# Mixture of experts between attention and a cosine MLP: second-layer product two blocks behind, PSUM split five and three, three float64 blocks in the last stage

## Chip, cores and metric

The kernel runs on one core of a Trainium2 chip. The metric is the device time of one execution in microseconds, the median over several runs. A separate profiled execution gives the trace.

## The reference, cut to what matters

Three layers one after the other: attention with a position bias, a mixture of eight experts of which every token uses two, and an MLP with a cosine gate. The last two are what the change touches.

```python
# x: 1152 tokens x 512, after attention
out = np.zeros((N, D), dtype=np.float32)
for e in range(E):                       # E = 8
    for k in range(2):
        mask = top2[:, k] == e
        h = np.maximum(x[mask] @ w1[e], 0.0)           # 512 -> 1024
        out[mask] += top2_w[mask, k, None] * (h @ w2[e])   # 1024 -> 512

def _moe2_ref(x, w_in, w_out):           # 512 -> 2048 -> 512, weights float64
    h = x @ w_in
    g = h * np.cos(h)
    return (g @ w_out).astype(np.float32)
```

## The kernel before, in words

**Stages.** Attention fills the first 240 us. Its tokens go to DRAM (`xg`) in eight slots of C = 320 rows, one slot for each expert. The function `experts` then does the experts' stage and the last stage. It exists in several copies for different numbers of tokens in the fullest expert; the one that ran uses W = 304 columns.

**Products.** Every matrix is split in two parts, a high part (hi) in the matmul's own 32-bit format (float32r) and a remainder (lo), and a product is three matmuls, hi x hi, hi x lo and lo x hi (`passes`, L990, matmul at L996). A split is a copy on ScalarE, which rounds, and a subtraction on VectorE or GpSimd. So each block of weights (128 x 1024) costs L1034 and L1036, each token tile L1100 and L1102, and the hidden layer L1125 and L1127 (`hhl`).

**Experts' stage.** A block is 128 of an expert's 1024 hidden units; 8 experts have 64 blocks. For block g, `ejobs` (L1111) makes l1, 12 matmuls into one PSUM bank H; relu and split into `hhl`; then l2, 12 matmuls that add into four banks Y, which hold the expert's 512 outputs for W tokens. l2 has priority g+1.5, one block behind l1. After the last block the four Y are transposed into the one tile `io` (L1147) and stored to DRAM (`yd`, L1151). The tokens of an expert come from `xg` into the same tile `io` (L1088), are transposed (L1097) and split into `xhl`, which has two buffers (`xjobs`, L1085). So `io` holds in turn the tokens of expert e+1, the result of e, the tokens of e+2.

**Weights.** `wjobs` (L1014) loads a block into one of three `raw` tiles and splits it into a `whl` tile, of which there are four: three that were split during attention (shown as `qt` in the rows) and one of its own.

**Last stage.** The tokens are three groups of three tiles of 128. For each group `mjobs` (L1196) goes over 16 blocks: m1 (12 matmuls of 384 columns into an H bank), the cosine on ScalarE and VectorE as a chain of seven instructions (L1236 to L1248), and m2 (three matmuls of 512 columns for each tile, into its Y bank), two blocks behind m1 (priority 2.5). Before a group, `cjobs` (L1156) gathers each token's two results with GpSimd, weighs and adds them, and transposes them through an H bank (L1185).

**The float64 blocks.** The weights of the last stage come as float64. `djobs` (L1040) loads a block of 1024 KB into the tile `r64`, of which there is one (L1045), and makes a float32 from the two words of each number, in two halves: a ScalarE copy (L1060), three VectorE instructions (L1062, L1064, L1066), then the split, L1068 on ScalarE and L1070 on VectorE or GpSimd. The first `NPRE` = 12 blocks are made during the experts' stage and kept in tiles `w64`; the other four are made in the last stage's first group, after the gathers of that group, into the `whl` tiles, and stay there for all three groups.

**Order.** Nothing is ordered by hand. `Plan` (L55) takes each operation with its engine or engines and a duration for each, a priority, and what it reads and writes, and places them as a list scheduler: of the operations that could start within 0.08 us of the earliest, the lowest priority number goes first, on the engine where it would end first. What has a limited number of buffers opens them in the order of priority (`turn`). The resulting order is the program's; on the chip each engine and each DMA queue runs its own list in that order and waits for semaphores. All loads and stores here are issued by the queue of SP but for GpSimd's gathers.

Of the kernel before, what the change touches and what calls it, by code (L numbers as in the profile page):

```python
# [8 lines left out]
F32 = mybir.dt.float32  # L9
# [10 lines left out]
DM = H * D  # L20
# [16 lines left out]
RAWS = 3  # L37
# [127 lines left out]
def attention_moe_cosine_mlp_kernel(  # L165
# [783 lines left out]
    def experts(bctx, W, ahead=True):  # L949

        pool = bctx.enter_context(tc.tile_pool(name="mlp", reuse_waits="tile", bufs=1))
        ps = bctx.enter_context(tc.tile_pool(name="ps", reuse_waits="tile", bufs=4, space=PSUM))
        bctx.enter_context(tc.manual_schedule())
        NPRE = 12
        FINE = {NFIRST: 1}
        DG, CF, CS = 2, 1, 3
        DP, FREE = 3, 0
        IDLE0, IDLE1 = 0, 0
# [6 lines left out]
        bufs = dict(Y=4, H=4, raw=RAWS, whl=4, xhl=2, hhl=3, io=1, r64=1, s=4, w=2, u=4)  # L965
# [3 lines left out]
        whls = wfirst + [pool.tile(sizes["whl"], F32R, name="whl")]  # L969
# [5 lines left out]
        def tl(tag, key):  # L975
            if (tag, key) not in live:
                if tag in "YH":
                    live[tag, key] = ps.tile([128, 512], F32, name=tag)
# [8 lines left out]
        def xhl(k, v):  # L987
            return xparts[k % 2][v]

# [24 lines left out]
        def wjobs(i, pr):  # L1014
# [6 lines left out]
            if i in FINE:  # L1021
                n = FINE[i]
                for a, c in [(0, c) for c in range(n)] + [(1, 0)]:
# [5 lines left out]
                    P.op({"DVE": 0.07 + 0.00104 * m, "POOL": 0.1 + 0.00225 * m}, (lambda a, sl: lambda e: (  # L1029
# [6 lines left out]
            P.op({"DVE": 1.135, "POOL": 2.0}, lambda e: (nc.gpsimd if e == "POOL" else nc.vector).tensor_tensor(  # L1036
# [3 lines left out]
        def djobs(f, pr, step, load_after=(), after=()):  # L1040
# [8 lines left out]
            for m in range(2):  # L1049
# [28 lines left out]
                P.op({"DVE": 0.602, "POOL": 1.25}, words(5), p + 0.05, r=[uk + (3,), wn + (0, m)], w=[wn + (1, m)])  # L1078
# [6 lines left out]
        def xjobs(e, pr):  # L1085
            ik = ("io", ("x", e))
            for i in range(4):
                xl.setdefault(e, []).append(P.op({"SP": 0.45}, (lambda i: lambda en: nc.sync.dma_start(  # L1088
                    tl(*ik)[32 * i:32 * i + 32].rearrange("p j c b -> p j (c b)"), blocked(xg, e, i)))(i),
                    pr - 2.5 - 2 + 0.01 * i, r=["xg"], w=[ik + (i,)], xfer=0.455))  # L1090
            for c in range(4):
# [3 lines left out]
                def part(u, c=c):  # L1095
# [3 lines left out]
                    pr - 2.5 + 0.4 * c, r=[ik + (i,) for i in range(4)], w=[sk])  # L1099
                P.op({"ACT": 0.093 + 0.00083 * W}, (lambda part, sk: lambda en: nc.scalar.activation(  # L1100
                    part(0), tl(*sk)[:, 0:W], AF.Copy))(part, sk), pr - 2.5 + 0.4 * c + 0.01, r=[sk], w=[xk + (0,)])
                P.op({"DVE": 0.402}, (lambda part, sk: lambda en: nc.vector.tensor_tensor(  # L1102
                    part(1), tl(*sk)[:, 0:W], part(0).bitcast(F32), op=OP.subtract))(part, sk),
                    pr - 2.5 + 0.4 * c + 0.02, r=[sk, xk + (0,)], w=[xk + (1,)])
# [6 lines left out]
        def ejobs(g):  # L1111
# [9 lines left out]
            for c0 in (0, 2):  # L1121
                ml1[-g] = P.op({"PE": 0.0025 * W}, l1(c0), g + 0.1 * c0, r=wuse(g, 0, (c0, c0 + 1))
                     + [("xhl", e, c, u) for c in (c0, c0 + 1) for u in range(2)], w=[pk + (c0,)], hold=[hk])
# [13 lines left out]
            for c in range(4):  # L1137
                P.op({"PE": 0.00125 * W}, l2(c), g + 1.5 + 0.01 * c, r=wuse(g, 1, (0,))
# [57 lines left out]
        def mjobs(g, f, pr):  # L1196
# [13 lines left out]
            for c0 in (0, 2):  # L1210
                ml1[g, f] = P.op({"PE": 0.0025 * N}, m1(c0), pr + 0.1 * c0 - (0 if (g, f) == (0, 0) else 0), r=[wn + (u, 0) for u in range(2)]
# [67 lines left out]
            for s in range(T):  # L1279
# [3 lines left out]
                for q in range(n):  # L1283
                    yk, c, d = ("Y", 4 * E + t + q), slice(DM // n * q, DM // n * (q + 1)), slice(0, DM // n)
                    P.op({"PE": 0.64 / n}, m2(s, yk, c, d), pr + 2.5 + 0.01 * s + 0.001 * q, r=[wn + (v, 1) for v in range(2)]
# [211 lines left out]
```

## Time and profile before

| what | value |
|---|---|
| median of 3 runs | 697.38 us (694.0 to 697.47) |
| profiled execution, its own time | 690.71 us |
| span of its trace | 688.9 us, 12810 instructions |
| TensorE busy | 634.7 us, 92% |
| VectorE busy | 505.3 us, 73% |
| ScalarE busy | 395.2 us, 57% |
| GpSimd busy | 137.0 us, 20% |
| mean granted TensorE clock | 0.981 of full speed |

The span runs from the first to the last instruction; 1.8 us lie around it. Busy shares are means over the stages. In the trace PE is TensorE's matmuls, PEld its weight loads, DVE VectorE, ACT ScalarE, POOL GpSimd, SP the queue that issues most DMAs. Ends of matmuls are modelled, so starts are the safer numbers.

### The profile page before, as it was taken

How to read it: one execution, taken by the hardware profiler on the slowest of the kernel's cores; microseconds unless marked ns; L12 is line 12 of the kernel's file. 1: busy time of each engine (PE TensorE's matmuls, PEld its weight loads, DVE VectorE, ACT ScalarE, POOL GpSimd, SP SyncE). 2: the span in 40 equal slices, each digit the busy share in tenths (PEclk: the TensorE clock that was granted, in tenths of full speed). 3: DMA queues.
4: the chain of work that ended last, by engine and by line, in shares of the span. 5: the costliest groups of instructions: out<-in, count | busy, mean ns of one | idle time of the engine just before them, and what ended most of it. 6: DMA issues, size and time to landing. Idle time of an engine off the chain costs nothing.

```text
span 688.9 us, 12810 instructions
## 1 busy us (share of the span) xinstructions
PE 634.7 (92%) x4678; PEld 552.6 (80%) x4678; DVE 505.3 (73%) x1256; ACT 395.2 (57%) x789; POOL 137.0 (20%) x196
## 2 busy tenths in 40 slices
PE   5778999999999859998999999999999999999996
PEld 1346676676688659998999998899999999999996
DVE  7796899999879529986888879556887545554543
ACT  5666688869668336664665656444664354334333
POOL 4140124332322202321122231022300040001000
PEclk9998999999999869999999999999999999999999
DMA  5858788776864358978798897874620040001001
GB/s 176 205 159 257 243 295 260 241 236 195 240 194 156 117 146 223 269 249 252 266 278 255 248 275 237 194 191 160 199 108 1 0 138 1 1 2 45 1 1 46
DMA packets 58177, 116.45 MB, mean 169 GB/s; under 512 B 7024, under 2 KB 26864, under 8 KB 56048
## 3 DMA queue, kind: packets, MB, share of 16 engines
q1 hardware_dynamic: 54544, 104.41, 51.2%
q0 software_dynamic: 3552, 11.04, 4.8%
q8 instruction: 41, 0.67, 0.4%
q14 instruction: 40, 0.33, 0.2%
HBM read 78.12 MB, written 32.58 MB: 161 GB/s over the span
## 4 chain that ended last, share of the span: by engine, by line
PE 33%; DMA 13%; DVE 13%; issue 4%; SPq 2%; ACT 1%; POOL 0%; DVEq 0%; ACTq 0%; POOLq 0%
PE Y L996 16%; PE H L996 16%; DMA yd<-io 5%; DMA io<-xg 5%; DVE qt L1036 3%; DVE hhl L1127 2%; DVE s L1097 1%; DVE io L1147 1%; DMA wraw<-yd,mixed 1%; SPq L1151 1%; DVE s L1064 1%; SPq L1088 1%; DVE s L1066 1%; DVE whl L1036 1%; DVE xnext L1102 1%
## 5 line engine op out<-in xcount | busy, mean ns | idle before, releaser
L996 PE MATMUL Y<-hhl,qt 128*128 128x304 f32 x576 | 93.3, 304 | 10.1 <-DVE hhl L1127 8.1
L996 PEld LDWEIGHTS Y<-hhl,qt 128*128 128x128 f32 x576 | 82.4, 188 | 15.5 <-DVE hhl L1127 12.4
L996 PE MATMUL Y<-w,hhl 128*128 128x512 f32 (+1 forms) x360 | 81.7, 372 | 0.0
L996 PEld LDWEIGHTS Y<-w,hhl 128*128 128x128 f32 x360 | 61.8, 188 | 9.5
L996 PE MATMUL H<-qraw,qt 128*128 128x304 f32 (+1 forms) x360 | 58.9, 314 | 8.2 <-ACT warm L1310 8.2
L1034 ACT ACTIVATE qt<-wraw 128x1024 fp32r<-128x1024 f32 x45 | 47.6, 1058 | 31.8 <-PE Y L996 26.0
L1070 POOL TENSOR_TENSOR w<-s,w 128x512 fp32r<-128x512 f32 x23 | 40.1, 1748 | 128.8 <-ACT w L1068 128.8
L502 ACT ACTIVATE e<-t,m 128x576 f32<-128x576 f32 x72 | 55.5, 771 | 13.3 <-DVE m L493 12.6
L996 PEld LDWEIGHTS H<-qraw,qt 128*128 128x128 f32 x360 | 55.4, 194 | 9.0 <-issue 8.5
L1036 DVE TENSOR_TENSOR qt<-wraw,qt 128x1024 fp32r<-128x1024 f32 x44 | 54.7, 1242 | 8.7 <-ACT qt L1034 8.6
L488 PE MATMUL S<-kt,qt 128*128 128x288 f32 x320 | 58.9, 313 | 1.1 <-DVE m L493 1.1
L493 DVE CUSTOM_DVE_ANT_0 t<-S,bias 128x576 f32<-128x576 f32 x72 | 53.5, 751 | 7.7 <-issue 2.9
L996 PE MATMUL H<-qraw,w 128*128 128x384 f32 x288 | 53.8, 335 | 0.0
L996 PEld LDWEIGHTS H<-qraw,w 128*128 128x128 f32 x288 | 50.8, 188 | 1.8
L996 PE MATMUL H<-xnext,qt 128*128 128x304 f32 (+1 forms) x324 | 50.4, 304 | 0.0
L488 PEld LDWEIGHTS S<-kt,qt 128*128 128x128 f32 x320 | 45.2, 190 | 6.4 <-issue 3.8
L509 PE MATMUL etp<-ident,e 128*128 128x128 f32 x288 | 44.6, 278 | 4.8 <-ACT e L502 4.1
L996 PEld LDWEIGHTS H<-xnext,qt 128*128 128x128 f32 x324 | 47.3, 188 | 0.3
L1236 ACT ACTIVATE u<-H 128x384 f32<-128x384 f32 (+1 forms) x52 | 23.8, 465 | 41.4 <-PE H L996 41.3
L537 PE MATMUL aux<-et,vt 128*64 128x128 f32 (+1 forms) x640 | 42.5, 277 | 4.0 <-DMA vt<-in_vd_dram 2.9
L1242 ACT ACTIVATE u<-u 128x384 f32<-128x384 f32 (+1 forms) x52 | 25.7, 499 | 35.7 <-DVE u L1240 35.7
L1248 DVE TENSOR_TENSOR hhl<-u,hhl 128x384 fp32r<-128x384 f32 (+1 forms) x52 | 27.3, 528 | 23.2 <-ACT hhl L1246 23.1
(205 smaller groups left out, 1272.5 us busy)
## 6 DMA issues: line engine op xcount, KB each, us to landing
wraw<-in_mwp_dram SPq DMA_DIRECT2D x64, 512.0 KB, 4.8
r<-in_mw2p_dram SPq DMA_DIRECT2D x16, 1024.0 KB, 7.1
dist<-bst SPq DMA_DIRECT2D x24, 295.5 KB, 3.7
bias<-dist SPq DMA_DIRECT2D x24, 288.0 KB, 4.3
xg<-zero SPq DMA_DIRECT2D x20, 256.0 KB, 4.7
yd<-zero SPq DMA_DIRECT2D x20, 256.0 KB, 5.0
yd<-io SPq DMA_DIRECT2D x32, 160.0 KB, 6.0
io<-xg SPq DMA_DIRECT2D x28, 160.0 KB, 5.4
```

What stands on the lines that cost most here:

```text
L488: nc.tensor.matmul(s[:, hf, 0:HF], tl("qt", (it, bb))[:, u, h, :], kt[:, bb, h, hf * HF:hf * HF + HF], start=(i == 0), stop=(i == len(term ...
L493: nc.vector.tensor_tensor_reduce(out=tl("t", n).rearrange("p (a j) -> p a j", a=2), in0=tl("S", n)[:, :, 0:HF], in1=tl("bias", it)[:, h, : ...
L502: P.op({"ACT": 0.76}, lambda e: nc.scalar.activation(tl(*ek)[:, 0:S], tl("t", n), AF.Exp, bias=tl("m", n), scale=-1.0, accum_out=tl("rs", ...
L509: nc.tensor.transpose(tl("etp", n)[:, j * 128:(j + 1) * 128], tl(*ek)[:, j * 128:(j + 1) * 128], ident)
L537: nc.tensor.matmul(tl(*ax2)[h0, q0], lw, rx, start=(s == 0), stop=(s == 4))
L996: nc.tensor.matmul(out_, lw(a), rx(b_), start=(first and i == 0), stop=(last and i == n - 1))
L1034: P.op({"ACT": 0.947}, lambda e: nc.scalar.activation(wt(i)[:, 0], tl(*rk), AF.Copy), pr, r=[rk], w=[wname(i) + (0,)])
L1036: P.op({"DVE": 1.135, "POOL": 2.0}, lambda e: (nc.gpsimd if e == "POOL" else nc.vector).tensor_tensor(wt(i)[:, 1], tl(*rk), wt(i)[:, 0].bi ...
L1070: (nc.gpsimd if e == "POOL" else nc.vector).tensor_tensor(wt(i)[:, 1, m], u, wt(i)[:, 0, m].bitcast(F32), op=OP.subtract)
L1236: P.op({"ACT": 0.06 + 0.00083 * m}, lambda e: nc.scalar.activation(u(), h(), AF.Copy, scale=1.0 / (2.0 * math.pi), bias=0.25), z, r=ks, w= ...
L1242: P.op({"ACT": 0.187 + 0.00083 * m}, lambda e: nc.scalar.activation(u(), u(), AF.Sin, scale=2.0 * math.pi), z + 0.04, r=[un[1]], w=[un[2]])
L1248: P.op({"DVE": 0.069 + 0.00104 * m}, lambda e: nc.vector.tensor_tensor(part(1), u(), part(0).bitcast(F32), op=OP.subtract), z + 0.07, r=[u ...
```

## The change

Second-layer products of the experts get priority g+2.5 in place of g+1.5. The eight PSUM banks are five Y and three H in place of four and four. `NPRE` falls from 12 to 9, so three more of the float64 blocks are made in the last stage. `whl` has FFB - NPRE = 7 buffers, four of its own, in place of 4; with nine `w64` tiles in place of twelve this takes the same SBUF. `hhl` gets four buffers for three, `u` three for four. The token work of an expert moves ahead by half a block (`XE` 3.0 in place of 2.5). The plan's durations change: a matmul of n columns counts 0.002 + 0.0004475 n us, and subtractions on GpSimd count more. These durations only decide the order and which engine takes a subtraction.

```diff
-        ps = bctx.enter_context(tc.tile_pool(name="ps", reuse_waits="tile", bufs=4, space=PSUM))
+        ps = bctx.enter_context(tc.tile_pool(name="ps", reuse_waits="tile", bufs=1, space=PSUM))
...
-        NPRE = 12
+        NPRE = 9
...
+        XE = 3.0
...
-        bufs = dict(Y=4, H=4, raw=RAWS, whl=4, xhl=2, hhl=3, io=1, r64=1, s=4, w=2, u=4)
+        bufs = dict(Y=5, H=3, raw=RAWS, whl=FFB - NPRE, xhl=2, hhl=4, io=1, r64=1, s=4, w=2, u=3)
...
-        whls = wfirst + [pool.tile(sizes["whl"], F32R, name="whl")]
+        whls = wfirst + [pool.tile(sizes["whl"], F32R, name=f"whl{i}") for i in range(bufs["whl"] - NFIRST)]
...
-                    live[tag, key] = ps.tile([128, 512], F32, name=tag)
+                    live[tag, key] = ps.tile([128, 512], F32, name=tag, bufs=bufs[tag])
...
+        def mm(n):
+
+            return 0.002 + 0.0004475 * n
...
-                    P.op({"DVE": 0.07 + 0.00104 * m, "POOL": 0.1 + 0.00225 * m}, (lambda a, sl: lambda e: (
+                    P.op({"DVE": 0.07 + 0.00104 * m, "POOL": 1.1 + 0.00127 * m}, (lambda a, sl: lambda e: (
...
-            P.op({"DVE": 1.135, "POOL": 2.0}, lambda e: (nc.gpsimd if e == "POOL" else nc.vector).tensor_tensor(
+            P.op({"DVE": 1.135, "POOL": 2.4}, lambda e: (nc.gpsimd if e == "POOL" else nc.vector).tensor_tensor(
...
-                P.op({"DVE": 0.602, "POOL": 1.25}, words(5), p + 0.05, r=[uk + (3,), wn + (0, m)], w=[wn + (1, m)])
+                P.op({"DVE": 0.602, "POOL": 1.75}, words(5), p + 0.05, r=[uk + (3,), wn + (0, m)], w=[wn + (1, m)])
...
-                    pr - 2.5 - 2 + 0.01 * i, r=["xg"], w=[ik + (i,)], xfer=0.455))
+                    pr - XE - 2 + 0.01 * i, r=["xg"], w=[ik + (i,)], xfer=0.455))
...
-                ml1[-g] = P.op({"PE": 0.0025 * W}, l1(c0), g + 0.1 * c0, r=wuse(g, 0, (c0, c0 + 1))
+                ml1[-g] = P.op({"PE": 6 * mm(W)}, l1(c0), g + 0.1 * c0, r=wuse(g, 0, (c0, c0 + 1))
...
-                P.op({"PE": 0.00125 * W}, l2(c), g + 1.5 + 0.01 * c, r=wuse(g, 1, (0,))
+                P.op({"PE": 3 * mm(W)}, l2(c), g + 2.5 + 0.01 * c, r=wuse(g, 1, (0,))
...
-                    P.op({"PE": 0.64 / n}, m2(s, yk, c, d), pr + 2.5 + 0.01 * s + 0.001 * q, r=[wn + (v, 1) for v in range(2)]
+                    P.op({"PE": 3 * mm(DM // n)}, m2(s, yk, c, d), pr + 2.5 + 0.01 * s + 0.001 * q, r=[wn + (v, 1) for v in range(2)]
```

The three priorities of L1099 to L1104 take XE in the same way, and m1 takes 6 * mm(N).

## Rows read from the trace of the kernel before

**Rows 1.** The page's chain that ended last, by engine.

```profile
PE 33%; DMA 13%; DVE 13%; issue 4%; SPq 2%; ACT 1%; POOL 0%; DVEq 0%; ACTq 0%; POOLq 0%
```

**Rows 2.** Windows: stretch, length, busy PE, PEld, DVE, ACT, POOL, clock, DMA.

```profile
392.35:420.85 28.50, 27.45 (x195) 26.57 (x193) 23.60 (x45) 17.45 (x28) 6.84 (x4) 1.00 0.89 267
480.05:549.00 68.95, 68.95 (x357) 62.87 (x356) 52.88 (x113) 36.82 (x76) 5.99 (x6) 1.00 0.25 79
```

**Rows 3.** Timeline of TensorE: start, length, instructions, idle time before.

```profile
249.01 5.40 PE L996 MATMUL H<-qraw,qt 128*128 128x304 f32 x24 [8.22 <-ACT warm L1310]
254.24 1.82 PE L996 MATMUL Y<-hhl,qt 128*128 128x304 f32 x12
...
392.35 1.82 PE L996 MATMUL H<-xnext,qt 128*128 128x304 f32 x12
394.00 1.82 PE L996 MATMUL Y<-hhl,whl 128*128 128x304 f32 x12
...
415.91 1.79 PE L996 MATMUL Y<-hhl,qt 128*128 128x304 f32 x11 [0.68 <-DVE hhl L1127]
...
420.85 1.81 PE L996 MATMUL H<-qraw,qt 128*128 128x304 f32 x12
...
480.05 6.40 PE L996 MATMUL H<-qraw,w 128*128 128x384 f32 x36
```

**Rows 4.** Waits, 246 to 480: us in total, times, longest.

```profile
ACT qt L1034 <- PE Y L996: 26.0, 22, 2.2
...
DVE s L1097 <- DMA io<-xg: 16.5, 5, 4.4
...
PE Y L996 <- DVE hhl L1127: 8.1, 14, 1.1
```

**Rows 5.** Timeline of the fifth expert: the round through io.

```profile
395.86 1.71 DVE L1147 STREAM_TRANSPOSE io<-Y 128x320 f32<-128x320 f32 x4
...
397.60 2.39 SPq L1151 DMA_DIRECT2D yd<-io  x4
...
405.73 1.84 SPq L1088 DMA_DIRECT2D io<-xg  x4
...
413.07 1.30 DVE L1097 STREAM_TRANSPOSE s<-io 128x320 f32<-128x320 f32 x3 [2.88 <-DMA io<-xg]
...
415.78 1.23 DVE L1102 TENSOR_TENSOR qraw<-s,qraw 128x304 fp32r<-128x304 f32 x3
...
418.84 0.46 DVE L1102 TENSOR_TENSOR qraw<-s,qraw 128x304 fp32r<-128x304 f32 x1
```

**Rows 6.** Timeline of the last stage; then all loads of r64 (first and last start).

```profile
487.25 10.29 SPq L1045 DMA_DIRECT2D r<-in_mw2p_dram  x2
493.22 0.65 ACT L1060 ACTIVATE w<-r 128x512 int32<-128x512 uint32 x1
493.82 0.75 DVE L1062 TENSOR_SCALAR s<-r 128x512 uint32<-128x512 uint32 x2
496.43 0.69 DVE L1064 SCALAR_TENSOR_TENSOR s<-r,s 128x512 uint32<-128x512 uint32 x1
540.55 2.27 PE L996 MATMUL H<-qraw,whl 128*128 128x384 f32 x12
...
L1045 SPq DMA_DIRECT2D r<-in_mw2p_dram x16: 327/352/1326, 249.6 to 507.9; - x16
```

**Rows 7.** Two lines: ns shortest/median/longest, first and last start.

```profile
L1066 DVE CUSTOM_DVE_ANT_0 s<-s,w x32: 674/684/2886, 260.5 to 521.3; 128x1024 uint16<-128x1024 uint16 x32
...
L1070 POOL TENSOR_TENSOR w<-s,w x23: 1282/1817/2276, 265.6 to 429.8; 128x512 fp32r<-128x512 f32 x23
L1070 DVE TENSOR_TENSOR qt<-s,qt x6: 677/690/694, 483.5 to 510.5; 128x512 fp32r<-128x512 f32 x6
```

**Rows 8.** Timeline: VectorE beside GpSimd.

```profile
260.42 2.39 POOL L1036 TENSOR_TENSOR qt<-wraw,qt 128x1024 fp32r<-128x1024 f32 x1 [17.51 <-ACT qt L1034]
260.47 2.89 DVE L1066 CUSTOM_DVE_ANT_0 s<-s,w 128x1024 uint16<-128x1024 uint16 x1
```

More of the change, by code (lines that the diff above doesn't have):

```diff
@@ L1098, in xjobs @@
                     tl(*sk)[:, 0:C].rearrange("p (j a) -> p j a", j=CJ), tl(*ik)[:, :, c, :]))(c, sk),
-                    pr - 2.5 + 0.4 * c, r=[ik + (i,) for i in range(4)], w=[sk])
+                    pr - XE + 0.4 * c, r=[ik + (i,) for i in range(4)], w=[sk])
                 P.op({"ACT": 0.093 + 0.00083 * W}, (lambda part, sk: lambda en: nc.scalar.activation(
-                    part(0), tl(*sk)[:, 0:W], AF.Copy))(part, sk), pr - 2.5 + 0.4 * c + 0.01, r=[sk], w=[xk + (0,)])
+                    part(0), tl(*sk)[:, 0:W], AF.Copy))(part, sk), pr - XE + 0.4 * c + 0.01, r=[sk], w=[xk + (0,)])
                 P.op({"DVE": 0.402}, (lambda part, sk: lambda en: nc.vector.tensor_tensor(
                     part(1), tl(*sk)[:, 0:W], part(0).bitcast(F32), op=OP.subtract))(part, sk),
-                    pr - 2.5 + 0.4 * c + 0.02, r=[sk, xk + (0,)], w=[xk + (1,)])
+                    pr - XE + 0.4 * c + 0.02, r=[sk, xk + (0,)], w=[xk + (1,)])
         def wuse(g, a, cs):
@@ L1210, in mjobs @@
             for c0 in (0, 2):
-                ml1[g, f] = P.op({"PE": 0.0025 * N}, m1(c0), pr + 0.1 * c0 - (0 if (g, f) == (0, 0) else 0), r=[wn + (u, 0) for u in range(2)]
+                ml1[g, f] = P.op({"PE": 6 * mm(N)}, m1(c0), pr + 0.1 * c0 - (0 if (g, f) == (0, 0) else 0), r=[wn + (u, 0) for u in range(2)]
                      + [("xhl", E + g, t, u) for t in range(T) for u in range(2)], w=[pk + (c0,)], hold=[hk])
```

## The prediction

> **What bounds the kernel now.** I read the chain of work that ended last first [rows 1]: TensorE leads it, but DMA and VectorE hold 13% each, and in order of time these shares lie in the experts' stage; behind it the chain is TensorE alone. So I read by stage. In the windows [rows 2] the fifth expert has TensorE busy 27.45 of 28.50 us and VectorE 23.60, while in the first third of the last stage TensorE is busy all of 68.95 us and VectorE 52.88. Of the change, the order of the second-layer product can win only in the experts' stage, and the moved conversions can lose only in the last one.
>
> The timeline of TensorE [rows 3] gives the size. Twelve matmuls of an expert's block start 1.65 us after the twelve before them (392.35 to 394.00). The stage starts at 249.01 and the last stage's first product at 480.05: 231.0 us. Its 64 blocks have 128 such groups, 211.6 us at 1.653; the first two take 5.23 in place of 3.31 (249.01 to 254.24), 1.9 more, and the three transposes put between them about 0.45 each, 1.3. That makes 214.8, so TensorE lost 16.2 us, some 2.3 in each of seven experts. One such place is in the rows: of a second-layer group one matmul goes ahead, and the other eleven start at 415.91, after 0.68 us of idle time put down to hhl on VectorE. The waits [rows 4] show that cause first on TensorE (8.1 us in 14 places). Behind it stands VectorE's own wait for the tokens of the next expert: 16.5 us in five places. An hhl subtraction queued behind such a wait is late, and TensorE with it.
>
> **The change part by part.** *Second layer two blocks behind.* Today l2(g) follows l1(g+1), so hhl has 1.65 us, one group, between the end of its first-layer product and its use. With g+2.5 it follows l1(g+2): l2(g-1) and a further l1 lie between, three groups, 4.96 us. All stalls put down to hhl in the rows are under that margin (1.1 us the longest by the waits' records), so this part alone gives back the 16.2 us. Three H banks do not take it back: l1(g+3) needs the bank of g, and l2(g), which stands before it, needs the same hhl. The fifth Y bank costs nothing and gives little: VectorE empties four banks in 1.71 us, beside a first-layer group of 1.65.
>
> *What is late next.* The io tile has one buffer. An expert's result goes Y, io, yd; then tokens for the expert after next go xg, io, xhl. In the fifth expert's rows [rows 5] the transposes out of Y start at 395.86, the four stores issue from 397.60, the loads only from 405.73, and the first transpose of the tokens runs at 413.07 after 2.88 us of waiting: 17.2 us of round trip. The first three parts are split by 417.01, the fourth by 419.30; l1 of that expert starts at 420.85, so 1.5 us were spare. Now between the last l2 of an expert and the l1 two experts on there are seven l1 and seven l2, 23.1 us. Two blocks behind, six and six are left: 19.8 us. From 395.65, where the fifth expert's last group, issued at 394.00, gives way, that is 415.5 for the first half of l1 and 416.3 for the second. In the order that VectorE has there, a weight subtraction and an hhl stand between the transposes, and the fourth part comes at 419.3, 3.0 us late. With the token work packed together (four transposes, a subtraction of 0.47 behind each) the first half is ready 2.2 us after landing, 415.3, and the last at 416.6, 0.3 late at most. XE 3.0 and the DVE work taken away push towards the second; that the store and the load share a queue with weight loads keeps the 17.2. I take 1.2 us for each of the six experts 2 to 7, 7.2 in all; ends 0 and 3.0 each, 0 and 18. Experts' stage: 16.2 - 7.2 = 9.0 us won, ends +16.2 and -1.8.
>
> *Seven whl buffers for four.* ScalarE waits 26.0 us in 22 places for TensorE to release a weight buffer [rows 4]. Those waits go, and an hhl or token copy behind them on ScalarE comes sooner. Without them two blocks behind would have to live on four buffers, three of which hold blocks in use. I price it as the cover of the 9.0, not on top of it.
>
> *Three float64 blocks out of the experts' stage.* A block is two halves of ScalarE copy, L1062, L1064, L1066, ScalarE rounding, and the subtraction L1070. On VectorE two L1062 take 0.75, L1064 0.69 and L1066 0.68 a half [rows 6, 7]: 3.5 us, 10.5 for three; the L1070 was on GpSimd 23 times of 24. That is 1.3 us an expert, room that VectorE needs: 23.60 of work and 2.88 of waiting already make 26.48, the 16 groups' 26.45. Hidden, so 0, but if it were not removed VectorE would be the bound. Three loads of r leave SP's queue here, and six L1070 leave GpSimd's, ahead of the gathers of the last stage.
>
> *The same blocks in the last stage.* Here L1070 was on VectorE (0.69), so a block costs 4.87 us, three 14.6. VectorE's idle time in the window is 68.95 - 52.88 = 16.1 [rows 2], so 1.5 us are left and the work fits only if it can be placed freely. It can't: r64 has one buffer. A load was issued at 487.25, ScalarE read it at 493.22, its last L1064 ended at 497.1, the next load left by 497.5, and the last one at 507.9 [rows 6]: (507.9 - 487.25) / 2 = 10.3 us a cycle. TensorE wants the last block at 540.55, 60.5 us into the stage. Seven blocks have one load ahead of the stage, the second at +7.2 as now, the seventh five cycles on. At 10.3 a cycle it is issued at +58.7, lands 6.0 on, and its first half is split 3.6 later (0.38 + 3 x 0.69, and an estimated 1.1 for ScalarE's rounding and the handovers): +68.3, 7.8 us late. With nothing between its own instructions a cycle is 6.0 + 0.75 + 1.38 + 0.5 = 8.6, the block is ready at +59.8, and nothing is lost. With VectorE this full I take 9.3: +63.3, 2.8 us late. H banks open in order, so no later product can fill that hole. The loads themselves cross an idle DMA (share 0.25 there, [rows 2]), and SP has nothing else to issue. Ends 0 and 7.8.
>
> *Prices in the plan.* The TensorE, GpSimd and VectorE figures change no instruction, only the order and who does a subtraction. GpSimd's dearer L1070 (median 1.82 us, [rows 7]) may send some of the 18 left to VectorE, 0.69 each; at half of them 0.8 us an expert, inside the 1.3 set free: 0, ends -1 and +1 in all. A DVE instruction beside a GpSimd one can be drawn out: L1066 took 2.89 us at 260.47, beside GpSimd's 2.39 us from 260.42, where its median is 0.68 [rows 7, 8]. By the Trainium skill, SBUF — State Buffer, "Who interferes with whom", an instruction of VectorE with two SBUF inputs is shut out for the whole of a GpSimd instruction that reads SBUF. By that rule six L1070 fewer on GpSimd would give VectorE up to 6 x 1.82 = 10.9 us more in the experts' stage; by the median of L1066, which is undisturbed, almost nothing, and I count nothing.
>
> Sum: 690.71 - 9.0 + 2.8 = 684.5 us for the profiled execution. The runs' median, 697.38, is 1% above that execution, so the forecast is 697.38 x 684.5 / 690.71 = 691.1.
>
> **Rivals.** *Nothing comes in place of the hhl stalls.* The token work is packed, the seven blocks are in time: 16.2 won, 0 lost, 681. For it: margin 4.96 against stalls of about 1. Against: the 17.2 us round trip does not shrink by itself. The skill's rule above would speak for this end.
>
> *The last stage takes it back.* The cycle of r64 stays at 10.3: 9.0 - 7.8 = 1.2 won, 696. For it: three loads in a row left at that pace. Against: late blocks have higher priority than the waves beside them. The same time comes out if the plan still places many l2 one block behind.
>
> *The io round trip sets the pace.* At 3.0 us or more late in each of six experts the stage is no faster than now: -18 + 16.2 = -1.8, and 2.8 more in the last stage; at 3.4, as long as VectorE's waits for io get, -4.2 and 2.8: 7.0 lost, 704. It decides against the change from 2.8 us late per expert on (6 x 2.8 + 2.8 = 16.2 + 3.4). For it: the rows' own order gives 3.0. Against: that order had 1.5 us to spare, and need not be kept.
>
> **How the numbers follow.** Forecast 0.42, at 691, own range 688 to 694; all of it won 0.18, at 681 to 685; taken back 0.20, at 694 to 699; io round trip 0.20, at 701 to 705. A measurement of this kernel can tell about 0.5%, 3.5 us, from no change. Faster 0.42 + 0.18 = 0.60, same 0.20, slower 0.20. The range is 681 to 703: the low end is the full 16.2, and above 703 lies the upper part of the last case.
>
> **What would show it.** Right: in the experts' stage no idle time of TensorE put down to hhl on VectorE in mid-expert; 26.5 to 28 us from one expert's first l1 to the next; what is left stands at the first l1 of experts 2 to 7, and is put down to the token split (L1102) or ScalarE's L1100. In the last stage a hole before the products of the last one or two converted blocks, put down to L1068 or L1070, of 0 to 8 us; r loads 8.6 to 10.3 us apart. Wrong: stalls on hhl as before, an expert of 29 us or more, or a second wave chain that is late because VectorE is full, which would stop TensorE in many places of the first third of the last stage.

## The result: 1% slower, 704.45 us

| | before | after |
|---|---|---|
| median | 695.89 us (694.0 to 697.47, 4 runs) | 704.45 us (701.83 to 706.47, 4 runs) |
| profiled execution | 690.71 us | 704.64 us |
| ratio | | 1.0101, 95% interval 1.0052 to 1.015 |

A second set of ten runs of the same changed kernel (c_after) gave 1.0065 (1.0024 to 1.0106). The forecast was 691.1 us, and its range ended at 703: both the direction and the range were wrong. In the changed kernel line numbers from L987 on are five higher (L996 is L1001, L1097 is L1102); the runs with a changed landing time, below, add one or two more.

The page's chain that ended last, by engine, of the changed kernel, answers to [rows 1]: TensorE falls from 33% to 28%, VectorE and DMA go from 13% each to 16 and 14.

```profile
PE 28%; DVE 16%; DMA 14%; issue 4%; ACT 2%; SPq 2%; DVEq 0%; POOL 0%; ACTq 0%; POOLq 0%
```

Windows of the changed kernel, an undisturbed stretch of the experts' stage and the first 68.95 us of the last stage, as in [rows 2]:

```profile
408.25:436.75 28.50, 28.46 (x207) 28.21 (x206) 18.61 (x34) 13.22 (x22) 0.00 (x0) 1.00 0.73 203
491.01:559.96 68.95, 67.12 (x345) 60.41 (x344) 63.01 (x131) 41.78 (x86) 12.31 (x9) 1.00 0.40 131
```

So the order two blocks behind can run without a gap: 28.46 of 28.50 us. And the moved blocks load VectorE in the last stage, 63.01 us for 52.88, with TensorE now idle there. The timeline of TensorE shows where the stalls are instead:

```profile
311.76 0.41 PE L1001 MATMUL H<-qraw,qt 128*128 128x304 f32 x1 [3.08 <-ACT qraw L1105]
313.16 1.64 PE L1001 MATMUL H<-qraw,qt 128*128 128x304 f32 x5 [0.99 <-DVE qraw L1107]
314.59 2.58 PE L1001 MATMUL Y<-hhl,qt 128*128 128x304 f32 x12
317.02 1.81 PE L1001 MATMUL H<-qraw,whl 128*128 128x304 f32 x12
...
491.01 6.41 PE L1001 MATMUL H<-qraw,w 128*128 128x384 f32 x36
...
549.22 2.35 PE L1001 MATMUL H<-qraw,whl 128*128 128x384 f32 x12 [1.61 <-DVE u L1249]
```

The waits of the changed kernel from 246 to 480, as in [rows 4]:

```profile
PE H L1190 <- DVE s L1184: 3.3, 1, 3.3
PE H L1001 <- ACT qraw L1105: 3.1, 1, 3.1
PE Y L1001 <- ACT whl L1039: 2.9, 1, 2.9
PE Y L1001 <- DVE io L1152: 1.8, 2, 1.3
PE Y L1001 <- DVE hhl L1132: 1.6, 2, 0.8
PE H L1001 <- DVE qraw L1107: 1.0, 1, 1.0
...
DVE s L1102 <- DMA io<-xg: 18.9, 6, 5.5
```

The 8.1 us for hhl [rows 4] are down to 1.6, as forecast. In their place come waits for tokens (L1105, L1107), for a weight split (L1039), for Y banks (L1152), and for the first tokens of the last stage (L1184). VectorE waits for token loads as long as before. Summed over the experts' stage, without the wait ahead of its first product, TensorE's idle time is 14.4 us, where it was 10.1.

The stages, read from the timeline of TensorE in every run below (experts: from the first 304-column product to the first 384-column one; last: from there to the end of the span), in us:

```
run            experts   last    ratio to before (95%)
before          231.04  208.85
c_before        236.53  208.89   0.9991 (0.9959 to 1.0023)
after           235.73  211.79   1.0101 (1.0052 to 1.0150)
c_after         236.58  211.77   1.0065 (1.0024 to 1.0106)
lag1            242.19  213.68   1.0226 (1.0167 to 1.0285)
lag2_only       238.57  209.25   1.0122 (1.0062 to 1.0182)
b_npre9         232.14  211.56   1.0041 (1.0010 to 1.0072)
b_npre9_lag2    231.57  212.80   1.0006 (0.9977 to 1.0036)
b_banks         231.94  214.03   1.0049 (1.0022 to 1.0076)
oldprices       230.86  215.64   1.0073 (1.0036 to 1.0110)
newprices       247.30  212.30   1.0222 (1.0140 to 1.0304)
newp_land       239.72  209.01   1.0041 (1.0015 to 1.0068)
after_land      224.66  225.59   1.0085 (1.0052 to 1.0117)
after_tok       234.92  214.05   1.0063 (1.0034 to 1.0093)
after_land2     226.40  212.86   0.9904 (0.9869 to 0.9938)
b_lag2_land     234.71  222.91   1.0256 (1.0208 to 1.0304)
b_lag2_tok      236.36  215.52   1.0108 (1.0064 to 1.0152)
b_io2           228.69  211.45   0.9979 (0.9956 to 1.0002)
b_io2_land      226.40  221.92   1.0055 (1.0024 to 1.0085)
io2             239.44  211.99   1.0195 (1.0163 to 1.0228)
```

Attention, untouched by the change, ends between 238.2 and 245.6 us in these twenty profiles, so single spans can't be compared, only stages and ratios. Each row's stages are of one profiled execution. The two rows of the kernel before differ by 5.5 us in the experts' stage, the two of the changed kernel by 0.9: a difference of a few us between two rows shows little by itself.

### The profile page after: what moved, and what is told of

Its sections match the earlier page's. It is cut to its first block, busy times and chain, and to the rows that moved or that the text cites. A ratio compares the mean times of both kernels' runs of the same rounds, so it can differ in the third digit from the quotient of the medians.

```text
span 702.8 us, 12811 instructions
## 1 busy us (share of the span) xinstructions
PE 640.8 (91%) x4678; PEld 556.5 (79%) x4678; DVE 509.0 (72%) x1268; ACT 393.0 (56%) x789; POOL 118.0 (17%) x184
## 4 chain that ended last, share of the span: by engine, by line
PE 28%; DVE 16%; DMA 14%; issue 4%; ACT 2%; SPq 2%; DVEq 0%; POOL 0%; ACTq 0%; POOLq 0%
PE H L1001 14%; PE Y L1001 13%; DMA io<-xg 4%; DMA wraw<-in_mwp_dram 3%; DMA yd<-io 3%; DVE whl L1041 2%; DVE s L1071 2%; DMA r<-in_mw2p_dram 2%; DVE s L1069 1%; DVE s L1102 1%; DVE qt L1041 1%; DVE io L1152 1%; DVE hhl L1132 1%; SPq L1093 1%; DMA wraw<-yd,mixed 1%
## 5 line engine op out<-in xcount | busy, mean ns | idle before, releaser
L1001 PE MATMUL Y<-hhl,whl 128*128 128x304 f32 x432 | 68.6, 305 | 6.8 <-ACT whl L1039 2.9
L1001 PEld LDWEIGHTS Y<-hhl,whl 128*128 128x128 f32 x432 | 62.6, 191 | 8.4 <-ACT whl L1039 3.8
L1001 PE MATMUL Y<-w,hhl 128*128 128x512 f32 (+1 forms) x270 | 60.8, 371 | 0.0
L1001 PEld LDWEIGHTS Y<-w,hhl 128*128 128x128 f32 x270 | 47.6, 188 | 7.9
L1001 PE MATMUL H<-qraw,whl 128*128 128x304 f32 (+1 forms) x312 | 51.3, 312 | 1.8 <-DVE u L1249 1.6
L1001 PE MATMUL H<-qraw,qt 128*128 128x304 f32 (+1 forms) x240 | 41.3, 323 | 12.4 <-issue 8.4
L1001 PE MATMUL Y<-hhl,qt 128*128 128x304 f32 x336 | 52.1, 303 | 0.1
L1001 PEld LDWEIGHTS H<-qraw,whl 128*128 128x128 f32 x312 | 47.3, 188 | 3.1 <-DVE u L1249 2.0
L1041 DVE TENSOR_TENSOR whl<-wraw,whl 128x1024 fp32r<-128x1024 f32 x33 | 41.3, 1252 | 10.7 <-ACT whl L1039 10.6
L1001 PEld LDWEIGHTS Y<-hhl,qt 128*128 128x128 f32 x336 | 48.7, 191 | 0.5 <-DVE hhl L1132 0.5
L1001 PEld LDWEIGHTS H<-qraw,qt 128*128 128x128 f32 x240 | 38.3, 197 | 13.4 <-issue 8.6
L1039 ACT ACTIVATE whl<-wraw 128x1024 fp32r<-128x1024 f32 x35 | 36.9, 1057 | 16.8 <-PE Y L1001 9.2
L509 PEld LDWEIGHTS etp<-ident,e 128*128 128x128 f32 x288 | 34.2, 145 | 13.4 <-ACT e L502 5.6
L537 PEld LDWEIGHTS aux<-et,vt 128*64 128x64 f32 x640 | 33.1, 143 | 12.9 <-issue 3.1
```

What stands on the lines that cost most here:

```text
L509: nc.tensor.transpose(tl("etp", n)[:, j * 128:(j + 1) * 128], tl(*ek)[:, j * 128:(j + 1) * 128], ident)
L537: nc.tensor.matmul(tl(*ax2)[h0, q0], lw, rx, start=(s == 0), stop=(s == 4))
L1001: nc.tensor.matmul(out_, lw(a), rx(b_), start=(first and i == 0), stop=(last and i == n - 1))
L1039: P.op({"ACT": 0.947}, lambda e: nc.scalar.activation(wt(i)[:, 0], tl(*rk), AF.Copy), pr, r=[rk], w=[wname(i) + (0,)])
L1041: P.op({"DVE": 1.135, "POOL": 2.4}, lambda e: (nc.gpsimd if e == "POOL" else nc.vector).tensor_tensor(wt(i)[:, 1], tl(*rk), wt(i)[:, 0].bi ...
```

## The experiments

### The two kernels once more

*c_before*: no edit. 

> The kernel before, unchanged, as a control. Attention is the same code in both kernels, yet its end came 6.1 us later in the profile of after (last transpose at 244.87 in place of 238.73). If that is scatter of single executions, this profile may end attention anywhere in 238 to 246, while the experts' stage stays at 231.0 us and the last one at 208.9, within 0.5 us each. Ratio 1.00.

*c_after*: no edit. 

> After, unchanged, as a control of its profile: attention may end anywhere in 238 to 246 us, the experts' stage 230 to 238 us, the last stage 211 to 212.5. If the stalls at the first token transpose of the last stage (4.5 us with its slow stretch) and at expert 2's first product (6) belong to the order of the program, both are there again, within 1.5 us.

The profiled execution that the forecast was built on, 690.71 us, lies 0.7% under the kernel's median: its experts' stage, 231.0 us, is 5.5 us shorter than that of c_before, where 231.0 within 0.5 was expected. Most of the 5.5 lies at one place, the third expert of c_before:

```profile
362.84 1.30 DVE L1097 STREAM_TRANSPOSE s<-io 128x320 f32<-128x320 f32 x3 [5.51 <-DMA io<-xg]
...
364.60 0.62 PE L996 MATMUL Y<-hhl,qt 128*128 128x304 f32 x1 [2.61 <-ACT hhl L1125]
```

VectorE stands 5.51 us before a token load, and TensorE stops for hhl behind it. At this place the first profile of the same program has a wait of 3.22 us on VectorE, and stops of only 0.32 and 0.68 on TensorE. So the kernel before, with its old durations, has this kind of stop too, in one execution and not in another.

The changed kernel repeats itself within 0.9 us in each stage. Against the mean of the two profiles of before (233.8 and 208.9) it loses 2.4 us in the experts' stage and 2.9 in the last one, 5.3 in all; 0.65 to 1.0% of 696 is 4.5 to 7.0.

### Which part of the change

*lag1*, the changed kernel with the old order of l2:

```diff
-                P.op({"PE": 3 * mm(W)}, l2(c), g + 2.5 + 0.01 * c, ...
+                P.op({"PE": 3 * mm(W)}, l2(c), g + 1.5 + 0.01 * c, ...
```

> After, with the second-layer product one block behind again, all else as in after. Theory A (results late: the lag takes one block, 3.3 us, from each road that an expert's result must go, by io to the next tokens and by the gather to the last stage): the stall of 4.9 us at the first token transpose of the last stage and the 6.0 us at expert 2's first product shrink below 1.5 each, the stalls on hhl come back (8 us or more), the experts' stage takes 228 to 236 us in place of 235.7. Theory B (the plan's new durations have put other work in front) and theory C (seven weight buffers and the moved blocks): both stalls stay, hhl stalls are added, 243 us or more.

Measured 1.0226, the experts' stage 6.5 us longer than in the changed kernel. So two blocks behind helps there, inside the change, and the first theory of the expectation, 228 to 236 us without it, fell. Something else in the change costs more than the order gives.

*lag2_only*, the kernel before with g + 2.5, `hhl=4` and `u=3`, so on four whl buffers. 

> Before, with the second-layer product two blocks behind and four hhl for three, three u for four (same memory); four whl buffers, twelve early blocks, four and four banks and the old durations stay. Theory A: hhl stalls go, a stall of 3 us or more comes at the token transposes of the last stage and at an expert's first product; experts' stage 228 to 238 us, not under 226. Theories B and C: nothing comes in place of the hhl stalls, 215 to 224 us. The last stage stays at 208.9 either way.

Measured 1.0122: the stage is 238.6 us, with TensorE held up by weight splits (L1036) ahead of an expert's first product. This agrees with the cover that the prediction named under the seven whl buffers. It does not isolate it: the run lacks the moved blocks as well as the buffers.

*b_npre9*, the kernel before with the blocks moved and the buffers for it:

```diff
-        NPRE = 12
+        NPRE = 9
-        bufs = dict(Y=4, H=4, ..., whl=4, ...
+        bufs = dict(Y=4, H=4, ..., whl=FFB - NPRE, ...
```

> Before, with nine early float64 blocks and seven whl buffers alone; lag 1, old durations, four and four banks. If moving the blocks costs what the last stage of after lost, the last stage takes 211 to 215 us in place of 208.9. If the room on VectorE (1.3 us an expert) is worth something, the experts' stage is 1 to 8 us under the 236.5 of the control; if only the lag can use it, it stays at 231 to 238. Theory D (the other parts, not the lag, made the kernel slower, as the run with lag 1 suggests): the whole is 5 us or more slower than before.

*b_npre9_lag2*, the same with g + 2.5, `hhl=4`, `u=3`. 

> The same with the second-layer product two blocks behind, hhl 4 and u 3: after without new durations, without XE 3.0 and with four and four banks. In the run with two blocks behind and four whl buffers the late thing was the weight split (L1036, 1.1 to 2.7 us before an expert's first product). With seven buffers these stalls should go: experts' stage 225 to 233 us, and the last stage as in the run with nine blocks alone. If it is no better than 235, the late weight split was not for want of buffers.

The moved blocks make the last stage 2.7 us longer (211.56); the order gives 0.35% back on top (1.0041 to 1.0006, intervals that overlap). Its stalls are tokens again: 1.54, 1.85 and 1.97 us at 306 to 319, put down to L1100 and L1102.

*b_banks*, that kernel with `Y=5, H=3`. 

> The kernel before with nine w64 blocks, seven whl buffers and the second product two blocks behind, and now five Y and three H banks as well; the lead of the tokens stays 2.5 and the plan's durations are the old ones, so against the run with the old durations only the lead of 3.0 is missing. If the three H banks cost the 0.7% between the two earlier runs (1.0006 and 1.0073), the time is 1.006 to 1.009 of before, the last stage 215 to 216 us, with waits for the u operations on VectorE ahead of its first products. If the lead of 3.0 costs it, the time is 0.999 to 1.002, the last stage 212 to 213.

*oldprices*, the changed kernel with the plan's durations of before, so b_banks with XE 3.0. 

> After, with all durations in the plan as in before (matmuls shorter, GpSimd's subtractions cheaper); XE stays 3.0. Theory A: the order changes in places, the two large stalls stay, experts' stage 233 to 239 us. Theory B: the stage comes back under 231 us, and at least one of the two large stalls goes. The last stage changes by less than 2 us from 211.8.

1.0049 and 1.0073: the longer last stage (214.0, 215.6) has one m1 waiting 2.81 and 2.85 us for the last reader of an H bank, `u` on VectorE (L1244, L1249). With four banks the same wait is 1.45 us. So the split five and three costs about 1 to 1.5 us, by one profile of each kernel; XE 3.0 lies inside the intervals.

oldprices also says what the new durations are worth inside the change. With the old ones the experts' stage is 230.86 us in place of 235.73, the last stage 215.64 in place of 211.79, and the ratio, 1.0073, lies between the two of the changed kernel, 1.0101 and 1.0065. To take the new durations back does not win the loss back. TensorE's idle time in the experts' stage of oldprices is 10.1 us, as much as in the kernel before, but for other things. Its waits from 255 to 492 us:

```profile
PE H L1001 <- DVE qraw L1107: 5.3, 3, 3.5
PE H L1190 <- DVE s L1184: 2.2, 1, 2.2
PE Y L1001 <- DVE io L1152: 1.2, 1, 1.2
...
PE Y L1001 <- DVE hhl L1132: 0.3, 1, 0.3
```

The waits for hhl are gone. Tokens (L1107), the first tokens of the last stage (L1184) and the emptying of Y (L1152) have taken their place.

*newprices*, the kernel before with the new durations and nothing else:

```diff
-                ml1[-g] = P.op({"PE": 0.0025 * W}, l1(c0), ...
+                ml1[-g] = P.op({"PE": 6 * (0.002 + 0.0004475 * W)}, l1(c0), ...
-                P.op({"PE": 0.00125 * W}, l2(c), g + 1.5 + 0.01 * c, ...
+                P.op({"PE": 3 * (0.002 + 0.0004475 * W)}, l2(c), g + 1.5 + 0.01 * c, ...
...
```

(and those of m1, m2, L1029, L1036 and L1070.) 

> Before, with the new durations of the plan alone. If the durations are what made after slower (theory B), the kernel is 5 us or more slower than before, and the waits behind hhl or the token work grow; if they are neutral or closer to the chip, within 3 us of before. Going from after to the old durations gave 231 for the experts and 215.6 for the last stage, so I expect the experts up by 0 to 6 and the last stage within 1.

This is a large effect for figures that no instruction reads: 1.0222, the experts' stage 247.3 us, beyond the 0 to 6 us expected. The new figures are the truer ones: twelve products of 304 columns count 1.66 us where the old formula gave 1.52 and the trace has 1.65 [rows 3], and L1070 on GpSimd counts 1.75 for 1.25, where its median is 1.82 [rows 7]. The work is the same. What differs is its order, and that ten of the 24 subtractions L1070 of the experts' stage have gone from GpSimd to VectorE (23 on GpSimd before, 13 here). The timeline of its third expert, all engines:

```profile
356.28 0.94 SPq L1088 DMA_DIRECT2D io<-xg  x2
...
360.59 1.81 PE L996 MATMUL H<-xnext,qt 128*128 128x304 f32 x12
363.00 0.91 DVE L1097 STREAM_TRANSPOSE s<-io 128x320 f32<-128x320 f32 x2 [5.59 <-DMA io<-xg]
363.55 0.46 ACT L1100 ACTIVATE qraw<-s 128x304 fp32r<-128x304 f32 x1 [4.63 <-DVE s L1097]
...
363.91 0.41 ACT L1125 ACTIVATE hhl<-H 128x304 fp32r<-128x304 f32 x1
...
364.37 0.40 PE L996 MATMUL Y<-hhl,qt 128*128 128x304 f32 x1 [1.97 <-ACT hhl L1125]
```

Read from the bottom: TensorE stops for hhl; ScalarE could not make it, since a token copy stands before it in order and waits 4.63 us for VectorE; VectorE stands 5.59 us before a transpose whose load, issued at 356.28, has not landed. It happens once in each of six experts, with 2.0 to 2.7 us of TensorE's time each.

### The landing time in the plan

The plan puts the bytes of all transfers one after another. One that finds none ahead of it counts as landed 0.65 us, its bytes' time and 1.25 us after its issue of 0.45: 2.8 us for a part of the tokens, 5.3 for an r64 load. The DMA view of the kernel before, 253 to 480 us, has the medians from issue to landing at the end of each line:

```profile
wraw<-in_mwp_dram SPq DMA_DIRECT2D x58, 512.0 KB, 4.8
r<-in_mw2p_dram SPq DMA_DIRECT2D x12, 1024.0 KB, 7.4
io<-xg SPq DMA_DIRECT2D x28, 160.0 KB, 5.4
yd<-io SPq DMA_DIRECT2D x28, 160.0 KB, 6.2
```

Those figures are too short by 2.6 for tokens and 2.1 for r64. Beside the issue and the bytes the plan counts 1.9 us; for a token load these rows leave 4.5, on DMA engines that are busy 0.82 of the stage. The Trainium skill, DMA: Bandwidth & Descriptors, "Anatomy of one DMA", gives a fixed cost of about 2.0 us for a transfer that GpSimd issues. These are issued by SP, and this trace has more than twice that figure for them.

*newp_land*: newprices, with the experts' plan told 2.75 us more for every transfer.

```diff
+    land = 1.25
-                end[i] = self.dma_free + 1.25
+                end[i] = self.dma_free + self.land
...
-        P = Plan(bufs, loose=("s",))
+        P = Plan(bufs, loose=("s",)); P.land = 4.0
```

> The kernel before with the new durations alone (1.0222 of before, experts' stage 247.3 us), and in the experts' plan a transfer counts as landed 4.0 us after its bytes are through where it was 1.25. If the durations harm because VectorE's token transposes come in order before their loads have landed, its waits for the token loads fall from 32.9 us under 12, the stage to 232 to 238, the time to 0.997 to 1.008 of before. If the durations themselves harm (GpSimd's share, the weight splits' order), the stage stays over 244 and the time over 1.015.

VectorE's waits for token loads, first in newprices:

```profile
DVE s L1097 <- DMA io<-xg: 32.9, 6, 6.3
```

and in newp_land:

```profile
DVE s L1098 <- DMA io<-xg: 6.9, 4, 2.7
```

The time went from 1.0222 to 1.0041 with the durations kept, and the six stalls on ScalarE's hhl are gone. The moved subtractions are not what cost: here even fewer L1070 are on GpSimd, 9 of 24. The stage, 239.7 us, is a little above what was expected; what is left there is tokens and weight splits.

*after_land*: the changed kernel with the same edit. 

> The changed kernel with only the plan's landing time of a transfer in the experts' part raised by the same 2.75 us. If the landing time is at fault, VectorE's waits for the token loads fall from 18.9 us under 8, the experts' stage from 235.7 to 228 to 231, and the time to 0.995 to 1.001 of before. If not, the stage stays at 234 to 237 and the time at 1.006 to 1.011.

The experts' stage fell by 11 us to 224.7, the shortest of all and more than expected, and VectorE's waits for token loads from 18.9 to 8.9. The last stage grew by 13.8, and the time with it. The timeline of TensorE there:

```profile
544.58 0.50 PE L1002 MATMUL Y<-whl,hhl 128*128 128x512 f32 x1 [2.26 <-DVE hhl L1254]
544.92 3.81 PE L1002 MATMUL H<-qraw,whl 128*128 128x384 f32 x12
...
554.99 0.51 PE L1002 MATMUL Y<-whl,hhl 128*128 128x512 f32 x1 [2.26 <-DVE hhl L1254]
555.34 3.81 PE L1002 MATMUL H<-qraw,qt 128*128 128x384 f32 x12
```

The stops stand at the products with converted blocks (whl).

*after_tok*: the changed kernel, with 4.0 for the token loads (L1093) and the output stores (L1156) alone, `xfer=(0.455, 4.0)`. 

> The changed kernel; the plan counts as landed 2.75 us later only the experts' token loads and output stores. If the token loads' place in VectorE's order is what the experts' stage lost, it goes to 224 to 229 us as with every transfer raised, and with a last stage of 211 to 213 the time is 0.983 to 0.993 of before. If the gain of the run with every transfer raised came from its other transfers (the f64 loads that VectorE and ScalarE wait for in order), the stage stays at 231 to 236 and the time at 0.999 to 1.009.

The theory that the tokens' place alone does it fell: VectorE's wait for them is almost gone, and the stage is no shorter (234.9). The waits of after_tok:

```profile
DVE s L1103 <- DMA io<-xg: 2.4, 3, 1.1
...
ACT w L1066 <- DMA r<-in_mw2p_dram: 11.4, 4, 3.6
```

Now TensorE itself waited for the tokens (2.44 and 1.49 us at 339 to 342, 1.34 and 1.95 at 371 to 376), and ScalarE still stood in order before r64 loads. The changed kernel shows what such a wait does. Its timeline, SP, VectorE and ScalarE:

```profile
292.09 0.76 SPq L1050 DMA_DIRECT2D r<-in_mw2p_dram  x1
294.08 2.38 SPq L1093 DMA_DIRECT2D io<-xg  x4
...
301.06 0.69 ACT L1065 ACTIVATE w<-r 128x512 int32<-128x512 uint32 x1 [5.27 <-DMA r<-in_mw2p_dram]
301.06 0.76 DVE L1067 TENSOR_SCALAR s<-r 128x512 uint32<-128x512 uint32 x2 [4.76 <-DMA r<-in_mw2p_dram]
...
310.72 0.89 DVE L1102 STREAM_TRANSPOSE s<-io 128x320 f32<-128x320 f32 x2
```

Both engines stood until 301.06 before an r64 load that took 9.0 us from its issue. The second pair of token transposes ran at 310.72, without any wait: their load was there, VectorE was not. TensorE stopped 3.08 us for them at 311.76.

*after_land2*: after_land, but the r64 loads of the seven blocks converted in the last stage keep 1.25.

```diff
-  ... mw2p[f].bitcast(U32)), pr - 2, w=[rk], xfer=2.92,
+  ... mw2p[f].bitcast(U32)), pr - 2, w=[rk], xfer=(2.92, 4.0 if f < NPRE else 1.25),
```

> The changed kernel with the landing time of every transfer in the experts' part raised by 2.75 us, but for the f64 loads of the seven blocks converted in the last stage, which keep 1.25. If those loads' planned lateness made the last stage 225.6 us, it goes back to 211 to 215, the experts' stage stays at 224 to 227, and the time is 0.986 to 0.992 of before, under both kernels. If the rest of the plan (tokens gathered, outputs stored late) made it long, the last stage stays over 220 and the time at 1.003 to 1.010.

687.39 us, 0.9904 (0.9869 to 0.9938): the experts' stage keeps its gain (226.4) and the last one is back at 212.9. It is the fastest kernel of the study. In the last stage 1.25 is also the truer figure. The DMA view of the kernel before, 480 to 540 us, with the DMA engines 0.28 busy:

```profile
r<-in_mw2p_dram SPq DMA_DIRECT2D x3, 1024.0 KB, 5.1
```

From issue to landing an r64 load took 5.1 us there and 7.4 in the experts' stage. The plan counts 5.3 with 1.25 and 8.0 with 4.0, so the runs with 4.0 for every transfer are wrong about the last stage. The waits of after_land2 on TensorE in the experts' stage:

```profile
PE H L1003 <- DVE qraw L1109: 3.0, 3, 1.7
PE H L1003 <- ACT qraw L1107: 1.3, 2, 1.0
PE H L1003 <- DVE qraw L1199: 0.9, 1, 0.9
PE Y L1003 <- DVE Y L1151: 0.7, 1, 0.7
PE Y L1003 <- DVE hhl L1134: 0.6, 1, 0.6
```

*b_lag2_land*: b_npre9_lag2 with 4.0 for every transfer. 

> The kernel before with nine w64 blocks, seven whl buffers and the second product two blocks behind (1.0006 of before), and the landing time raised by 2.75 us. If tokens that VectorE waits for in order (19.8 us) are what is left of its stalls, the experts' stage falls from 231.6 by 4 to 8 us and the time to 0.989 to 0.995. If the loads are late whatever the order, since the single io buffer frees late, the waits move from VectorE to TensorE and the time stays at 0.998 to 1.004.

*b_lag2_tok*: b_npre9_lag2 with 4.0 for tokens and stores. 

> The same for the kernel before with nine w64 blocks, seven whl buffers and the second product two blocks behind, on its old durations (1.0006 of before; with every transfer raised 1.0256, stages 234.7 and 222.9). If true durations and a true landing time belong together, the old short durations with the late tokens give late tokens: the stage stays at 231 to 236, the last at 212 to 214, the time 0.998 to 1.010. If the token loads' place is the whole matter, the stage falls to 225 to 229 here too and the time to 0.986 to 0.994.

The gain expected of the first did not come, 1.0256; the second, 1.0108, came out a little beyond the range of its first theory. In the first most of the loss is in the last stage, 222.9 us, where 4.0 is the wrong figure, as in after_land. The experts' stage is 3.1 and 4.8 us longer than in b_npre9_lag2. So on the old, too short durations the longer landing time did harm here, where on the new ones it took 11 us off the stage. Short transfers and short products look like two errors of the plan that made up for each other. The two kernels also differ in their PSUM split and XE, and b_io2_land, below, does not fit.

### The single io buffer

*b_io2*: b_npre9_lag2 with `io=2`, paid for by `hhl=3, s=3`, and the token loads due 5.5 blocks ahead in place of 4.5. 

> The kernel before with nine w64 blocks, seven whl buffers, the second product two blocks behind, and two io buffers (three hhl and three s buffers pay for the room), the load of an expert's tokens asked for half a lead earlier, 5.5 blocks ahead and not 4.5. If VectorE's waits in order for the token loads (19.8 us in the run without it) and the late tokens behind them (about 10 us of TensorE's stalls) come from the single io buffer, which holds a load back until the output before it is stored, VectorE waits less than 6 us and the experts' stage falls from 231.6 us by 6 to 10; the time is 0.985 to 0.992 of before. If the loads are late because of the transfer itself or of what it shares with, VectorE still waits over 12 us and the time stays 0.998 to 1.003.

*b_io2_land*: b_io2 with 4.0 for every transfer. 

> The kernel before with nine w64 blocks, seven whl buffers, the second product two blocks behind, two io buffers (0.9979 of before) and the landing time raised by 2.75 us. With both, no load should be late and none waited for in order: VectorE's waits for token loads from 9.9 us to under 3, the experts' stage from 228.7 to 222 to 227, the time 0.985 to 0.994 of before. If the late Y evacuations that this version already showed (1.85 us at 320) are the price of two buffers, the time stays at 0.996 to 1.001.

*io2*: the changed kernel with `io=2, hhl=3, s=3` and loads due 6 blocks ahead. 

> The changed kernel with the same two io buffers, three hhl and three s buffers, and the load one half of a lead earlier (5 + 1 blocks ahead). If the new durations harm because they move VectorE's token transposes ahead of loads that a single buffer holds back, the wait of 18.9 us on VectorE falls under 6, the experts' stage falls from 235.7 to 226 to 230, and the time is 0.995 to 1.001 of before. If the durations harm in another way (GpSimd's or ScalarE's order), the stage stays at 234 to 237 and the time at 1.006 to 1.011.

b_io2 halved VectorE's wait (19.8 to 9.9 us) and took 2.9 us off the stage, less than hoped; it equals the kernel before (0.9979). In b_io2_land the experts' stage is 226.4, 2.3 us less, though its durations are the old ones, and the last one 221.9, the same kind of loss as in after_land. In io2 the wait stayed (19.3 us) and Y banks were emptied late (L1149, 1.25 to 2.14 us once in each of five experts): 1.0195. So the second buffer did not help the changed kernel, whose plan reckons with its loads too early. Why the Y banks came late stays open.

## Why the prediction was wrong, point by point

- *Two blocks behind.* Right that the waits for hhl go: 9.5 us before (L1125 and L1127), 1.6 in the changed kernel, 0.3 in oldprices. Where nothing disturbs it the stage has no gap. Wrong that this alone gives back 16.2 us: only 10.1 of them were idle time in that trace, and they were read from one execution. The next profile of the same kernel has 5.5 us more there.
- *What is late next.* The sum came near, 7.2 us forecast and under 7 measured, but by luck. It was to be 1.2 us at each of six experts. It was 6.0 at expert 2 (311 to 317, with the low clock behind the stops) and under 1 at expert 3. Two more roads of an expert's result are late by the order two blocks behind and had no term: the last stage's first tokens (L1184, 3.3 us, none before) and the emptying of Y (L1152 and L1149, 2.2 us, 0.5 before).
- *Seven whl buffers* as the cover: lag2_only agrees, but does not isolate them.
- *Three H banks do not take it back; the fifth Y bank costs nothing.* No wait in the experts' stage is put down to the H banks' number. In the last stage they cost about 1 to 1.5 us.
- *Three float64 blocks out, hidden, 0.* b_npre9 does not speak against it: its stage, 232.1 us, lies between the two profiles of before. What remains of the blocks still stands in order before r64 loads, ScalarE for 10.8 us in 4 places, where it was 8.7 in 7.
- *The same blocks in the last stage.* 2.9 us for 2.8, again by luck. Of the seven loads the last five left 9.5 us apart in the mean, near the 9.3 assumed. But the second left at 489.92, 1.1 us ahead of the stage and not 7.2 into it, so no weight split was late. An H bank was (1.61 us at 549.22), behind a VectorE that was full as forecast.
- *Prices in the plan: 0, ends -1 and +1.* Wrong. Alone they cost 2.2% (newprices). Inside the change they cost 4.9 us in the experts' stage and gave 3.9 in the last (oldprices against the changed kernel).

**The step that failed is the experts' term, 9.0 us won with ends +16.2 and -1.8, and what it took for free is the plan's order.** Measured are 4.7 us lost by the two profiled executions, 2.4 by the means of two profiles each. The term priced hhl by its margin and the tokens by their round trip, took the token work to be packed together, and put the plan's new figures at 0. But VectorE and ScalarE run in order, and an instruction put ahead of its load holds up all behind it, as the rows of newprices show. The new durations are 4.9 us of the miss. Without them the stage is at 230.9 to 231.9 us (oldprices, b_banks, b_npre9_lag2), where 222.0 was forecast. A longer landing time in the plan changes the order and moves a few subtractions from GpSimd to VectorE; the work stays the same. It takes the changed kernel's stage from 235.7 us to 224.7 and 226.4. So what the plan decides is the cause of most of the miss.

In after_land2 the time is 0.9904 (0.9869 to 0.9938), and the forecast's own ratio was 691.1 / 697.38 = 0.9910. So a gain of that size was there to be had from the same change with another order. That the two figures meet is partly luck: against the means of before this kernel wins 7.4 us in the experts' stage and loses 4.0 in the last, where 9.0 and 2.8 were forecast.

The rival on the io round trip (704 us) had the time, but not the mechanism: it had the tokens 3 us or more late in each of six experts, some 18 in all.

Open is which transfers need the longer figure: tokens alone do not do it, and whether r64 alone would, or the weights too, was not tried. Open too is whether 4.0 works because it is truer, or because it makes another order that happens to be good. Only 1.25 and 4.0 were tried, and the orders of this study put the experts' stage anywhere from 224.7 to 247.3 us.

## What to carry to other kernels

A duration in a list scheduler's table is a change to every engine's order: price it by what stands behind each in-order wait, and change one table entry alone on the chip before calling it free. Errors of such a table may make up for each other, so try true compute times together with the issue-to-landing times that the DMA view shows, stage by stage: an r64 load took 7.4 us in one stage and 5.1 in the next. And take the size of a stall from more than one execution.

## What the runs showed of the hardware

A stop of TensorE can cost more than its idle time. In newprices it waited 2.70 us at 425 to 428, and 0.46 more; the timeline has the next two groups, of eleven and twelve products, at 3.16 and 2.86 us, where twelve usually take 1.81:

```profile
428.26 0.62 PE L996 MATMUL Y<-hhl,qt 128*128 128x304 f32 x1 [2.70 <-ACT hhl L1125]
429.35 3.16 PE L996 MATMUL Y<-hhl,qt 128*128 128x304 f32 x11 [0.46 <-DVE hhl L1127]
432.30 2.86 PE L996 MATMUL H<-xnext,qt 128*128 128x304 f32 x12
435.00 1.81 PE L996 MATMUL Y<-hhl,qt 128*128 128x304 f32 x12
```

and the windows over it have the granted clock (before the last two columns) at 0.53, that is near the lower of the two levels, 1.2 of 2.4 GHz, and then back at 1.00:

```profile
429.50:434.90 5.40, 5.40 (x23) 5.40 (x24) 5.40 (x12) 3.25 (x6) 0.00 (x0) 0.53 0.64 190
434.90:440.00 5.10, 5.10 (x39) 5.10 (x39) 4.89 (x8) 2.95 (x5) 1.62 (x1) 1.00 0.36 109
```

A first group of 2.95 us (429.35 to 432.30) and a second of 2.70 (to 435.00) against 1.65 each: 2.3 us on top of the 3.2 idle. Not every stop has this behind it. In the changed kernel the clock was 1.00 behind a wait of 1.61 us (window 549.20 to 556.00), and also behind one of 2.94 us for a weight split (window 385.77 to 390.80). What sets the two kinds apart was not found. The spread of attention's end, 238.2 to 245.6 us with the same instructions, was not explained.
